# A list scheduler orders all steps of an attention-and-two-MLP kernel; weight splitting and three remainders change engines

## The chip, the cores and the metric

The kernel runs on one core of a Trainium2 chip. The core has engines that each work through an instruction queue of their own, in order: TensorE (PE in the rows; its weight loads are PEld), VectorE (DVE), ScalarE (ACT), GpSimd (POOL) and SyncE (SP, which here only issues DMAs). Semaphores tie the queues together. The metric is the device time of one execution in microseconds (us). The profile gives one execution in detail; its span runs from the first to the last instruction.

## The reference, cut to what matters

```python
# q (1, 12288, 128), kv (1, 384, 32, 128), w_sr (128, 128)
kv_pool = kv.reshape(B, H // r, r, W // r, r, C).mean(axis=(2, 4))      # r = 4
k = v = kv_pool.reshape(B, -1, C) @ w_sr                                 # 768 rows of 128
s = (1.0 / np.sqrt(C)) * (q @ k.transpose(0, 2, 1)); s = s - s.max(-1, keepdims=True)
a = np.exp(s); a /= a.sum(-1, keepdims=True) + 1e-09
x = (a @ v).astype(np.float32).reshape(12288, 128)
h = x @ w_in;  g = np.where(h > 0, h, np.exp(np.minimum(h, 0)) - 1);  x = g @ w_out    # layer 1
h = x @ w_in2; g = np.maximum(0.01 * h, h);                           out = g @ w_out2  # layer 2
```

Both hidden widths are 2048. The weights of the layers are 64-bit floats in the inputs; the kernel reads them as pairs of 32-bit words.

## The kernel before

**Precision.** Every matmul is done three times: each operand is split into a head (a rounded `fp32r` copy) and a tail (the rest), and `mm3` (lines 78 to 81) adds head*head, head*tail and tail*head in PSUM. So each tensor that goes into a matmul has a head (`qh`, `eh`, `xh`, `gh`, `wh`) and a tail (`ql`, `el`, `xl`, `gl`, `wl`), and each tail is a subtraction on VectorE or GpSimd.

**Tiling.** The 12288 rows of q are 24 chunks of 512 columns. For a chunk, four tiles of 128 rows go through `scores` (six matmuls of 384 columns into one PSUM place), the maximum on VectorE, `expo` on ScalarE, `norm` on GpSimd, a write to a DRAM scratch and a read back (`d<-e`, `x<-d`), `turn` (a transpose in blocks on VectorE), and `split_e` (head on ScalarE, tail `el` on GpSimd). Then `values` runs 18 matmuls of 512 columns, and `split_x` makes the chunk's input of layer 1.

A chunk's layer is 8 units of 256 hidden columns. A unit is `up` (six matmuls into a PSUM place of two banks), the activation, `tail`, and `down` (six matmuls that add into the chunk's output bank `py`). In layer 1 the activation is two passes on ScalarE (`r`), then `elu` on VectorE (`g`), which frees the PSUM place, then a head `gh` on GpSimd; in layer 2 it is two passes on ScalarE (`gh` and `g`). `tail` is a subtraction on VectorE in both. There are 384 units. Three PSUM places (`bank2`, one pool of three) serve scores, values and ups in turn; `gl` has three buffers.

**Weights.** 32 blocks of 256 columns are turned from double words into heads and tails by ten steps: a clamp on GpSimd, five bit operations on VectorE, two copies on ScalarE, three products and sums on GpSimd (`split_w`, lines 185 to 232).

**Order.** A tick is one unit. At each tick the loop at the end emits, in a fixed order, `up(n)`, `elu(n-1)`, tails, a share of the weights' steps (all spread over the first `WT = 40` ticks), what the tables `side` and `prod` hold for that tick, the activation, and the `down` of an earlier unit (`LAG`). Units of the two layers alternate from `D2 = 13` units on. Each engine's queue is the order in which this loop emits. Loads go through SP's queue.

## Time and profile before

| what | value |
|---|---|
| median of 3 runs | 1629.83 us (1627.02 to 1638.85) |
| the profiled execution | 1628.08 us, span 1626.3 us |
| TensorE (PE) busy | 1385.2 us, 85% of the span |
| VectorE (DVE) busy | 1200.6 us, 74% |
| ScalarE (ACT) busy | 981.9 us, 60% |
| GpSimd (POOL) busy | 657.1 us, 40% |
| granted TensorE clock, mean | 0.946 |

The first row is the time to be compared, the second the execution from which all rows come; 1.8 us of it lie outside the span. A busy share is a mean over a start that is filled with weight splitting and a long regular stretch, so the stages are to be read apart. A matmul's busy time overlaps the next one's, so the pace of matmuls is read from their starts.

### The profile page before, as it was taken

What the parts mean: (1) busy time and instruction counts of PE and PEld (TensorE: products, weight loads), DVE (VectorE), ACT (ScalarE), POOL (GpSimd) and SP (SyncE); (2) the same over time, 40 slices, a digit from 0 to 9 for tenths busy, and PEclk for the clock granted to TensorE, in tenths of its full rate; (3) what the DMA queues carried; (4) which work ended last, traced back from release to release, by engine and by line L of the source; (5) the groups of instructions that cost most, each with busy time, mean ns of one, the idle gap of its engine ahead of it and who ended that gap; (6) DMA issues with size and microseconds to landing.
All of it is one profiled execution on the core that took longest, in us unless ns stands there. A gap on an engine that the chain in (4) does not pass through costs nothing.

```text
span 1626.3 us, 16605 instructions
## 1 busy us (share of the span) xinstructions
PE 1385.2 (85%) x5688; PEld 1092.7 (67%) x5688; DVE 1200.6 (74%) x1255; ACT 981.9 (60%) x1211; POOL 657.1 (40%) x542
## 2 busy tenths in 40 slices
PE   4356677988998998998999899899899899889998
PEld 3235456766776776776777777677677677767786
DVE  7788877767768778777777677777777777677764
ACT  2343455656657567566566566666666666666665
POOL 3676666334334344343343343443343343343210
PEclk9568788999999999999999899999999999999999
DMA  7432221121121221221221112212222222111100
GB/s 228 126 88 73 71 76 59 55 63 56 55 72 46 65 72 46 66 70 47 65 67 51 55 56 66 60 56 65 52 65 65 53 65 65 46 59 56 36 7 13
DMA packets 176035, 103.91 MB, mean 64 GB/s; under 512 B 105168, under 2 KB 158544, under 8 KB 175952
## 3 DMA queue, kind: packets, MB, share of 16 engines
q1 hardware_dynamic: 174752, 102.66, 22.1%
q8 instruction: 46, 0.75, 0.2%
q10 hardware_dynamic: 1200, 0.20, 0.1%
q14 instruction: 37, 0.30, 0.1%
HBM read 58.79 MB, written 44.04 MB: 63 GB/s over the span
## 4 chain that ended last, share of the span: by engine, by line
PE 48%; DVE 25%; issue 8%; ACT 6%; DMA 2%; POOL 1%; DVEq 0%; SPq 0%; POOLq 0%; ACTq 0%
DVE gl L495 10%; PE ps L79 9%; DVE g L485 8%; PE ps L81 8%; PE ps L80 8%; PE py L80 6%; PE py L79 6%; PE ps L417 6%; PE py L81 5%; DVE nm L354 3%; ACT gh L480 2%; ACT g L481 2%; DMA d<-e 1%; DVE e L395 1%; ACT qh L146 1%
## 5 line engine op out<-in xcount | busy, mean ns | idle before, releaser
L495 DVE TENSOR_TENSOR gl<-g,gh 128x1024 fp32r<-128x1024 f32 x384 | 613.9, 1614 | 351.7 <-ACT g L481 180.2
L489 POOL TENSOR_SCALAR gh<-g 128x1024 fp32r<-128x1024 f32 x192 | 244.0, 1271 | 543.1 <-DVE g L485 506.8
L79 PE MATMUL py<-gh,wh_o 128*128 128x512 f32 x768 | 310.6, 404 | 0.0
L80 PE MATMUL py<-gl,wh_o 128*128 128x512 f32 x768 | 309.6, 403 | 0.0
L81 PE MATMUL py<-gh,wl_o 128*128 128x512 f32 x768 | 308.4, 402 | 0.0
L480 ACT ACTIVATE gh<-ps 128x1024 fp32r<-128x1024 f32 x192 | 196.1, 1021 | 145.1 <-PE ps L81 143.1
L404 POOL TENSOR_TENSOR el<-e,eh 128x768 fp32r<-128x768 f32 x96 | 198.9, 2072 | 174.7 <-ACT eh L403 174.7
L485 DVE SCALAR_TENSOR_TENSOR g<-r,ps 128x1024 f32<-128x1024 f32 x192 | 231.8, 1207 | 10.0 <-ACT r L475 10.0
L360 ACT ACTIVATE e<-ps,nm 128x768 f32<-128x768 f32 x96 | 86.3, 899 | 244.5 <-DVE nm L354 237.3
L79 PE MATMUL ps<-xh,wh_i 128*128 128x512 f32 x384 | 165.5, 431 | 70.5 <-DVE g L485 64.5
L474 ACT ACTIVATE r<-ps 128x1024 f32<-128x1024 f32 x192 | 197.2, 1027 | 33.6 <-PE ps L81 33.6
L475 ACT ACTIVATE r<-r 128x1024 f32<-128x1024 f32 x192 | 203.8, 1062 | 6.1
L481 ACT ACTIVATE g<-ps 128x1024 f32<-128x1024 f32 x192 | 195.8, 1020 | 0.0
L79 PE MATMUL ps<-x2h,wh_i 128*128 128x512 f32 x384 | 154.1, 401 | 42.1 <-DVE g L485 42.1
L81 PEld LDWEIGHTS py<-gh,wl_o 128*128 128x128 f32 x768 | 148.7, 194 | 35.9
L79 PEld LDWEIGHTS py<-gh,wh_o 128*128 128x128 f32 x768 | 150.8, 196 | 32.1
L80 PEld LDWEIGHTS py<-gl,wh_o 128*128 128x128 f32 x768 | 149.2, 194 | 31.7
L80 PE MATMUL ps<-xl,wh_i 128*128 128x512 f32 x384 | 158.7, 413 | 1.1 <-DVE xl L426 1.1
L81 PE MATMUL ps<-xh,wl_i 128*128 128x512 f32 x384 | 158.4, 413 | 0.0
L79 PEld LDWEIGHTS ps<-xh,wh_i 128*128 128x128 f32 x384 | 76.3, 199 | 117.0 <-PE ps L81 48.1
L81 PE MATMUL ps<-x2h,wl_i 128*128 128x512 f32 x384 | 153.9, 401 | 0.0
L80 PE MATMUL ps<-x2l,wh_i 128*128 128x512 f32 x384 | 153.0, 398 | 0.0
(69 smaller groups left out, 1749.0 us busy)
## 6 DMA issues: line engine op xcount, KB each, us to landing
d<-e SPq DMA_DIRECT2D x96, 384.0 KB, 2.5
x<-d SPq DMA_DIRECT2D x96, 384.0 KB, 3.0
qn<-in_q_dram SPq DMA_DIRECT2D x96, 64.0 KB, 2.4
kv<-in_kv_dram SPq DMA_DIRECT2D x12, 512.0 KB, 8.4
out_dram<-y SPq DMA_DIRECT2D x94, 64.0 KB, 2.7
ws<-in_moe_w_in_dram SPq DMA_DIRECT2D x16, 256.0 KB, 2.8
ws<-in_moe_w_out_dram SPq DMA_DIRECT2D x16, 256.0 KB, 2.9
out_dram<-y ACTq DMA_DIRECT2D x2, 64.0 KB, 2.5
```

The lines of the kernel that those rows point to most:

```text
L79: nc.tensor.matmul(ps, w_hi, x_hi, start=start, stop=False)
L80: nc.tensor.matmul(ps, w_hi, x_lo, start=False, stop=False)
L81: nc.tensor.matmul(ps, w_lo, x_hi, start=False, stop=stop)
L404: nc.gpsimd.tensor_tensor(out=lo, in0=e, in1=f(hi), op=ALU.subtract)
L417: nc.tensor.matmul(ps, w, x, start=(i == 0), stop=(i == NMM - 1))
L474: nc.scalar.activation(out=r, in_=ps_u[n], func=AF.Relu, scale=-1.0)
L475: nc.scalar.activation(out=r, in_=r, func=AF.Exp, scale=-1.0)
L480: nc.scalar.activation(out=gh_u[n], in_=ps, func=AF.Prelu, alpha=0.01)
L481: nc.scalar.activation(out=g_u[n], in_=ps, func=AF.Prelu, alpha=0.01)
L485: nc.vector.scalar_tensor_tensor(out=g_u[n], in0=r_u.pop(n), scalar=-1.0, in1=ps_u.pop(n), op0=ALU.add, op1=ALU.max)
L489: nc.gpsimd.tensor_scalar(out=gh_u[n], in0=g_u[n], scalar1=1.0, scalar2=0.0, op0=ALU.mult, op1=ALU.add)
L495: nc.vector.tensor_tensor(out=gl_u[n], in0=g_u.pop(n), in1=f(gh_u[n]), op=ALU.subtract)
```

## The change

All work is written down as steps: an engine, an assumed length, the steps that it comes after, buffers that it takes and gives, and a key (roughly the unit at which it is wanted). A loop in the kernel's Python then keeps an assumed clock for each engine, always emits the step that can begin first (the lower key at equal times, no key more than `REACH = 12` beyond the oldest step left), and so fixes each engine's queue. The three PSUM places are pools of one buffer each, and the loop picks the place that its clock says is free first.

With it: of a weight block's steps, the mask and the product that VectorE did before the shift go; a magnitude (`w_abs`) on ScalarE stands ahead of the clamp, which now bounds from both sides, so VectorE has three operations a block where it had five. Four weight buffers are loaded ahead instead of two. `el` and `ql` are subtracted on VectorE instead of GpSimd. For the first two chunks (`NEARLY = 2`) TensorE transposes the tiles into PSUM and there is no trip through DRAM. `LAG` of layer 2 is 4 (was 3), `D2` is 12, `y` has one buffer (was two), `sums` two (was three).

```diff
-LAG = {1: 4, 2: 3}
-WT = 40
+WS = 4
+D2 = 12
+NEARLY = 2
+LAG = {1: 4, 2: 4}
+AHEAD = 28
+WAHEAD = 6
+REACH = 12
...
-        nc.gpsimd.tensor_tensor(out=lo_v, in0=x, in1=f(hi_v), op=ALU.subtract)
+        nc.vector.tensor_tensor(out=lo, in0=qx.pop(c), in1=f(hi), op=ALU.subtract)
...
-        nc.vector.tensor_scalar(
-            out=u(m), in0=u(v), scalar1=0x7FFFFFFF, scalar2=None, op0=ALU.bitwise_and
-        )
-        yield
-        nc.vector.scalar_tensor_tensor(
-            out=v, in0=m, scalar=LEAST, in1=v, op0=ALU.is_ge, op1=ALU.mult
-        )
+            nc.scalar.activation(out=v, in_=f(wst[i][:, :, 1]), func=AF.Abs)
+            nc.gpsimd.tensor_scalar(
+                out=v, in0=v, scalar1=TOP, scalar2=LEAST, op0=ALU.min, op1=ALU.max
+            )
...
+    def turn_early(t, slot):
+        ps = slot.rearrange("p b n -> p (b n)")
+        e = e_t.pop(t)
+        for b in range(NKB):
+            nc.tensor.transpose(ps[:, b * P:(b + 1) * P], e[:, b * P:(b + 1) * P], ident)
+        e_t[t] = ps[:, :NK].rearrange("p (b s i) -> p b i s", s=S, i=G)
...
+    def tail_e(t):
+        hi, lo = place(t)
+        nc.vector.tensor_tensor(out=lo, in0=e_t.pop(t), in1=f(hi), op=ALU.subtract)
-        nc.gpsimd.tensor_tensor(out=lo, in0=e, in1=f(hi), op=ALU.subtract)
...
+            el = step(DVE, 1.3, lambda n=n: elu(n), [xe], n + 1)
+            gh = step(POOL, 1.1, lambda n=n: elu_head(n), [el], n + 1.5)
+            take(el, "g", n, 3)
+            take(gh, "gh", n, 4)
+            give(el, "ps", u0)
+            both = [el, gh]
...
+                se = step(SP, 0.4, lambda t=t: send(t), [no], key + 3)
+                fe = step(SP, 0.4, lambda t=t: fetch(t), [se], key + 4)
+                tu = step(DVE, 1.0, lambda t=t: turn(t), [fe, av_done.get(c - 1)], key + 5.5)
...
+        tl = chain["tail"] = step(DVE, 1.25, lambda n=n: tail(n), [*both, chain["tail"]], n + 2)
+        take(tl, "gl", n, 3)
...
+    LATE = {ACT: 0.2, DVE: 0.1, POOL: 0.15, PE: 0.25, SP: 4.0}
...
+    while left_n:
+        while begun[left[front][1]]:
+            front += 1
+        horizon = left[front][0] + REACH
+        best = None
+        for e in range(5):
+            for key, i in waiting[e]:
+                if key > horizon:
+                    continue
+                t = can_begin(i)
+                if t is None:
+                    continue
+                t = max(t, ready[i], free_at[e])
+                rank = (max(t, free_at[e] + 0.25), key, i)
+                if best is None or rank < best[0]:
+                    best = rank, t, e, i
```

On VectorE, in the regular stretch, a unit's `elu` (it writes `g`) and the subtractions `gl` stood like this before; the numbers are the buffers, so a `g` can be followed to its `gl`:

```order
L485 SCALAR_TENSOR_TENSOR g_4770<-r_4748,ps_4727 128x1024
L495 TENSOR_TENSOR gl_4785<-g_4775,gh_4774 128x1024
L495 TENSOR_TENSOR gl_4787<-g_4770,gh_4772 128x1024
L354 TENSOR_REDUCE nm_4799<-ps_4792 128x1
L485 SCALAR_TENSOR_TENSOR g_4820<-r_4789,ps_4778 128x1024
L395 STREAM_TRANSPOSE e_4824<-x_4746 128x4x6x32
L495 TENSOR_TENSOR gl_4840<-g_4830,gh_4829 128x1024
L495 TENSOR_TENSOR gl_4842<-g_4820,gh_4822 128x1024
```

The same engine and stretch in the changed kernel:

```order
L402 STREAM_TRANSPOSE e_5055<-x_4865 128x4x6x32
L475 SCALAR_TENSOR_TENSOR g_5066<-r_5041,ps_5032 128x1024
L422 TENSOR_TENSOR el_4846<-e_5055,eh_4845 128x6x128
L402 STREAM_TRANSPOSE e_5086<-x_4999 128x4x6x32
L362 TENSOR_SCALAR ss_5061<-ss_5061 128x1
L363 RECIPROCAL rs_5097<-ss_5061 128x1
L495 TENSOR_TENSOR gl_5102<-g_5066,gh_5072 128x1024
L515 TENSOR_TENSOR x2l_5092<-py_4655,x2h_5091 128x512
L422 TENSOR_TENSOR el_4846<-e_5086,eh_4845 128x6x128
L495 TENSOR_TENSOR gl_5131<-g_5084,gh_5074 128x1024
L475 SCALAR_TENSOR_TENSOR g_5141<-r_5108,ps_5077 128x1024
L347 TENSOR_REDUCE nm_5151<-ps_5117 128x1
```

The subtraction `el` has come into VectorE's queue, and the distance from a `g` to its own `gl` is no longer fixed. Over the whole program the two rows straight behind an `elu` are both `gl` in 67 of 192 places before and in 31 now.

On GpSimd, in the first part of the program (weights of layer 1 and the attention of the first chunks), a stretch read like this before:

```order
L404 TENSOR_TENSOR el<-e,eh 128x6x128
L180 TENSOR_SCALAR v<-ws 128x256
L404 TENSOR_TENSOR el<-e,eh 128x6x128
L227 TENSOR_TENSOR v<-v,m 128x256
L228 TENSOR_TENSOR a<-a,wh_o_1_71 128x256
L229 TENSOR_TENSOR wl_o_1_72<-a,v 128x256
L180 TENSOR_SCALAR v<-ws 128x256
L404 TENSOR_TENSOR el<-e,eh 128x6x128
```

And now, with the same kind of work:

```order
L197 TENSOR_SCALAR v<-v 128x256
L373 TENSOR_SCALAR x<-e,rs 128x768
L197 TENSOR_SCALAR v<-v 128x256
L231 TENSOR_TENSOR v<-v,m 128x256
L373 TENSOR_SCALAR x<-e,rs 128x768
L235 TENSOR_TENSOR a<-a,wh_i_1_63 128x256
L239 TENSOR_TENSOR wl_i_1_64<-a,v 128x256
```

`el` is gone from the queue, and the steps of two blocks stand interleaved. Up to the last weight's tail GpSimd's queue held 128 weight steps, 20 `gh`, 15 `norm`, 14 `el` and 5 `ql` before; now it holds 128 weight steps, 19 `gh` and 16 `norm`. VectorE's queue up to the same block held 160 weight steps before and holds 96 now, with 24 `gl`, 19 `elu`, 17 maxima, 15 `el`, 7 `turn`.

On TensorE, at the end of the first chunk's attention, the order now is:

```order
L88 MATMUL ps_509<-kt_lo_96,qh_420 128x384
L89 MATMUL ps_509<-kt_hi_95,ql_421 128x384
L433 MATMUL ps_530<-eh_438,v_hi_93 128x512 x6
L433 MATMUL ps_530<-eh_438,v_lo_94 128x512 x3
L413 MATMUL ps_551<-ident_60,x_542 128x128 x6
L433 MATMUL ps_530<-eh_438,v_lo_94 128x512 x3
L433 MATMUL ps_530<-el_439,v_hi_93 128x512 x6
```

The six `ident` matmuls are one tile's transposes (48 in all, for eight tiles); between the two halves of `values` before there were scores, and no transposes at all.

## Rows read from the trace of the kernel before

**Rows 1.** Stretches (length, busy and count of each engine, granted clock, DMA).
```profile
0.00:274.50 274.50, 159.26 (x549) 123.73 (x550) 219.65 (x320) 114.78 (x197) 172.11 (x189) 0.78 0.34 104
274.50:1626.30 1351.80, 1225.93 (x5141) 968.93 (x5139) 980.94 (x936) 867.15 (x1015) 485.01 (x354) 0.98 0.20 56
400.00:1400.00 1000.00, 901.95 (x3774) 712.35 (x3775) 742.08 (x713) 642.93 (x761) 379.60 (x276) 0.98 0.21 60
1500.00:1560.00 60.00, 59.55 (x256) 47.42 (x255) 43.31 (x40) 42.11 (x46) 16.36 (x14) 1.00 0.11 31
```
**Rows 2.** Instruction groups on VectorE, 400 to 1400 us (busy us, mean ns, idle before).
```profile
L495 DVE TENSOR_TENSOR gl<-g,gh 128x1024 fp32r<-128x1024 f32 x259 | 431.0, 1678 | 247.5 <-PE py L80 128.4 <-ACT g L481 116.3 <-PE py L81 1.9
L485 DVE SCALAR_TENSOR_TENSOR g<-r,ps 128x1024 f32<-128x1024 f32 x130 | 156.8, 1206 | 0.0
L395 DVE STREAM_TRANSPOSE e<-x 128x768 f32<-128x768 f32 x65 | 63.2, 972 | 8.1 <-DMA x<-d 8.1
L354 DVE TENSOR_REDUCE nm<-ps 128x1 f32<-128x768 f32 x65 | 61.8, 951 | 0.0
```
**Rows 3.** Waits, 400 to 1400 us (who for whom, total, times, longest).
```profile
DVE gl L495 <- PE py L80: 128.4, 66, 4.3
DVE gl L495 <- ACT g L481: 116.3, 91, 3.3
PE ps L79 <- DVE g L485: 98.4, 94, 3.8
```
**Rows 4.** Timeline of TensorE without a gap: first and last of twelve matmuls.
```profile
704.72 0.40 PE L79 MATMUL py<-gh,wh_o 128*128 128x512 f32 x1
...
707.28 0.39 PE L81 MATMUL py<-gh,wl_o 128*128 128x512 f32 x1
```
**Rows 5.** Timeline of GpSimd and VectorE, 703 to 713 us (start, length).
```profile
703.28 1.06 POOL L489 TENSOR_SCALAR gh<-g 128x1024 fp32r<-128x1024 f32 x1 [4.87 <-DVE g L485]
...
707.11 4.02 DVE L495 TENSOR_TENSOR gl<-g,gh 128x1024 fp32r<-128x1024 f32 x2 [2.53 <-ACT g L481]
707.88 2.16 POOL L404 TENSOR_TENSOR el<-e,eh 128x768 fp32r<-128x768 f32 x1 [1.28 <-ACT eh L403]
...
712.43 1.22 DVE L495 TENSOR_TENSOR gl<-g,gh 128x1024 fp32r<-128x1024 f32 x1
712.69 1.87 POOL L489 TENSOR_SCALAR gh<-g 128x1024 fp32r<-128x1024 f32 x1 [0.23 <-DVE g L485]
```
**Rows 6.** Timeline of the start: first weight block, first `values`.
```profile
27.09 0.28 DVE L197 TENSOR_SCALAR m<-v 128x256 uint32<-128x256 uint32 x1
27.41 0.42 DVE L201 SCALAR_TENSOR_TENSOR v<-m,v 128x256 f32<-128x256 f32 x1
30.05 0.72 POOL L227 TENSOR_TENSOR v<-v,m 128x256 f32<-128x256 f32 x1 [6.01 <-DVE m L197]
72.18 1.65 PE L417 MATMUL ps<-eh,v_hi 128*128 128x512 f32 x3 [21.88 <-ACT eh L403]
```
**Rows 7.** Instruction groups of the whole run: weights, `norm`, small matmuls.
```profile
L180 POOL TENSOR_SCALAR v<-ws 128x256 f32<-128x256 f32 x32 | 15.9, 499 | 12.7 <-DMA ws<-in_moe_w_in_dram 5.7 <-DMA ws<-in_moe_w_out_dram 4.9
L227 POOL TENSOR_TENSOR v<-v,m 128x256 f32<-128x256 f32 x32 | 25.8, 806 | 7.5 <-DVE m L197 6.0 <-ACT v L216 1.5
L373 POOL TENSOR_SCALAR e<-e,rs 128x768 f32<-128x768 f32 x96 | 89.9, 937 | 133.9 <-issue 92.8 <-DVE rs L371 37.0 <-ACT r L475 3.6
L212 DVE SCALAR_TENSOR_TENSOR a<-v,a 128x256 uint32<-128x256 uint32 x32 | 25.7, 803 | 0.7
L207 DVE TENSOR_SCALAR a<-v 128x256 uint32<-128x256 uint32 x32 | 21.3, 664 | 0.7
L298 PE MATMUL ps<-pool_m,s 128*128 128x128 f32 x48 | 10.6, 361 | 11.9 <-DVE s L292 11.7
```
**Rows 8.** The exchange through DRAM: DMA issues (count, KB each, median us to landing).
```profile
d<-e SPq DMA_DIRECT2D x96, 384.0 KB, 2.5
x<-d SPq DMA_DIRECT2D x96, 384.0 KB, 3.0
```

More of the change, by code (lines that the diff above doesn't have):

```diff
@@ L232, in split_w @@
-        return rest
-    def split_all():
-        done = None
-        clamp(0)
-        for i in range(len(wjobs)):
-            done = yield from split_w(i, done)
-            yield
-        done()
-    wsteps = split_all()
-    nw = 5 * len(wjobs) + 1
-    wdone = [0]
-    def weights(n, part):
-        due = min(nw, -(-nw * (2 * n + part) // (2 * WT)))
-        while wdone[0] < due:
-            next(wsteps, None)
-            wdone[0] += 1
-    with tc.tile_pool(name="kvp", bufs=1) as kvp, tc.tile_pool(name="sums", bufs=3) as sum_p:
+        return w_abs, w_bound, w_shift, w_sign, w_power, w_low, w_head, w_b, w_rest, w_tail
@@ L255, in pooled_attention_elu_leaky_kernel @@
+    with tc.tile_pool(name="kvp", bufs=1) as kvp, tc.tile_pool(name="sums", bufs=2) as sum_p:
         wsr = kvp.tile([P, C], F32, name="wsr")
@@ L587, in pooled_attention_elu_leaky_kernel, with step, take, give @@
-    assert not later and not side and not prod
+    steps = []
+    takes, gives = {}, {}
+    def step(engine, length, do, after, key):
+        steps.append((engine, length, do, [a for a in after if a is not None], key))
+        return len(steps) - 1
+    def take(i, pool, n, bufs, put=None):
+        takes.setdefault(i, []).append((pool, n, bufs, put))
+    def give(i, pool, n):
+        gives.setdefault(i, []).append((pool, n))
+    PE, DVE, ACT, POOL, SP = range(5)
+    where = {}
+    firsts = {}
@@ new lines, in pooled_attention_elu_leaky_kernel @@
+    LATE = {ACT: 0.2, DVE: 0.1, POOL: 0.15, PE: 0.25, SP: 4.0}
+    count = len(steps)
+    needs = [len(s[3]) for s in steps]
+    feeds = [[] for _ in steps]
+    for i, s in enumerate(steps):
+        for a in s[3]:
+            feeds[a].append(i)
+    ready = [0.0] * count
+    waiting = [[] for _ in range(5)]
+    for i in range(count):
+        if not needs[i]:
+            waiting[steps[i][0]].append((steps[i][4], i))
+    left = sorted((s[4], i) for i, s in enumerate(steps))
+    front = 0
@@ new lines, in pooled_attention_elu_leaky_kernel, with can_begin @@
+    begun = [False] * count
+    free_at = [0.0] * 5
+    order = {}
+    free_from = {}
+    PLACES = 3
+    places = [0.0] * PLACES
+    place_of = {}
+    order["ws"] = list(range(WS))
+    order["e"] = [("q", 0)]
+    free_from["e", ("q", 0)] = 0.0
+    order["qn"] = [0, 1]
+    free_from["qn", 0] = 0.0
+    def can_begin(i):
+        t = 0.0
+        for pool, n, bufs, put in takes.get(i, ()):
+            if pool == "ps":
+                open_ = [x for x in places if x is not None]
+                if not open_:
+                    return None
+                t = max(t, min(open_))
+            else:
+                owners = order.setdefault(pool, [])
+                if len(owners) >= bufs:
+                    x = free_from.get((pool, owners[-bufs]))
+                    if x is None:
+                        return None
+                    t = max(t, x)
+        return t
@@ new lines, in pooled_attention_elu_leaky_kernel @@
+    left_n = count
+    while left_n:
[14 more added lines that the diff above has]
+                    best = rank, t, e, i
+        assert best, "no step can begin"
+        _, t, e, i = best
+        engine, length, do, _, key = steps[i]
+        waiting[e].remove((key, i))
+        begun[i] = True
+        left_n -= 1
+        for pool, n, bufs, put in takes.get(i, ()):
+            if pool == "ps":
+                p = min((x, k) for k, x in enumerate(places) if x is not None)[1]
+                places[p] = None
+                place_of[i] = p
+                put(ps_p[p].tile([P, 2, CH], F32, tag="s", name="ps"))
+            else:
+                order[pool].append(n)
+        do()
+        end = t + length
+        free_at[e] = end
+        seen = end + LATE[e]
+        for pool, n in gives.get(i, ()):
+            if pool == "ps":
+                places[place_of[n]] = seen
+            else:
+                free_from[pool, n] = seen
+        for k in feeds[i]:
+            needs[k] -= 1
+            same = steps[k][0] == e and e != SP
+            ready[k] = max(ready[k], end if same else seen)
+            if not needs[k]:
+                waiting[steps[k][0]].append((steps[k][4], k))
```

504 lines of the change are left out of this document (287 added, 217 removed).

## The prediction

> **What bounds the kernel now.** First the stretches [rows 1]. The run falls into two. Up to 274.5 us, about where the last weight block is finished, TensorE gets through 549 matmuls with busy time 159 us. In the other 1351.8 us it gets through 5141. In the middle of that long part it is the busiest engine, with 902 us in 1000 against VectorE's 742. That share flatters it, because busy times of neighbouring matmuls overlap. Its pace comes from starts without a gap: eleven matmuls of 512 columns in 707.28 - 704.72 = 2.56 us, 0.2327 us each [rows 4]; for 384 columns I take three quarters, 0.1745 us (an estimate by columns). A chunk has 192 matmuls of its 16 units, 18 of `values` and 24 narrow ones of `scores`: 210 x 0.2327 + 24 x 0.1745 = 53.1 us if TensorE never stops. From 400 to 1400 us there are 259 `gl`, 16 a chunk, so 16.2 chunks, 61.7 us each [rows 1, 2]. TensorE runs at 86% of its pace, and 8.6 us a chunk are stalls.
>
> Then who makes it stop. TensorE waits 98.4 us for VectorE's `g`, whose end frees a PSUM place; VectorE waits 128.4 us for TensorE, whose `down` frees a `gl` buffer, and 116.3 us for layer 2's `g` from ScalarE [rows 3]. So the two busiest engines stop each other in turn, though VectorE has work for only 742 of 1000 us: the order of the queues costs the time, not the amount of work. One piece of work does cost: two `gl` take 4.02 us together while GpSimd's `el` runs from 707.88 to 710.04 us, where one alone takes 1.22 us. A `gl` that starts while `el` is on ends about 1.1 us after it. The reverse shows too: `gh` takes 1.06 us alone and 1.87 us when a `gl` began 0.26 us before it [rows 5]. Over the 259 `gl` the mean is 1.678 us, 0.46 above the lone one [rows 2].
>
> **The start.** Both kernels must get 32 weight blocks done and the first chunks through. I measure it to the last weight's tail, and count each queue up to there. VectorE first. Three weight operations cost 0.28 + 0.42 + 0.28 = 0.98 us a block with GpSimd quiet [rows 6], 0.664 + 0.803 + 0.664 = 2.13 us at the run's means [rows 7]: 31 to 68 us. The 24 `gl` at 1.22 to 1.678 us are 29 to 40 us. The 19 `elu` at 1.206 are 23 us, the 17 maxima at 0.951 are 16 us [rows 2]. No row has `el` on VectorE. Its nearest is `gl`, the same subtraction with 1024 columns, so 0.92 to 1.26 us by columns (a gain is excluded, it is new work there): 14 to 19 us for 15. Seven `turn` at 0.97 are 7 us. The short ones and the pieces of 512 columns are some 14 us, an estimate by columns from `gl`. Sum: 134 to 187 us, from 27.1 us on. The two operations that leave VectorE were worth 32 x (0.664 + 0.803) = 47 us at the same means. GpSimd: 32 x (0.499 + 3 x 0.806) = 93 us, 19 `gh` at 1.06 to 1.87 us are 20 to 36 us, 16 `norm` at 0.937 are 15 us, so 128 to 144 us from about 30 us [rows 5 to 7]. VectorE is the longer of the two. Before, VectorE was busy 219.65 of the 274.5 us, 80%, because the ticks doled the weight steps out evenly while the engines waited for each other. With steps taken as they become ready I take 90% busy, between that 80% and full, and the middle of the sum, 160 us: 27 + 160/0.9 = **205 us**. With the low sum it is 175, with the high one 235.
>
> The rest of the start hides. The magnitudes on ScalarE are 32 passes of 256 columns: at GpSimd's 0.72 us for that shape 23 us, and ScalarE was busy for 115 of 274.5 us. If it were the late one, each block would be later by that pass. The 48 transposes cost TensorE between 0.06 us each (a quarter of 0.2327) and 0.361 us [rows 7], 3 to 17 us, while it idles for over 100 us there. They take away four to eight trips through DRAM; the first `values` waited 21.88 us for `eh` at 72.18 us [rows 6]. I count no extra gain, since the weights set the end of the start. Two more weight loads stand ahead of the second chunk's q in SP's queue; q is wanted after the first chunk's scores, so this is nothing, or 2 or 3 us if these loads are slow. One `y` buffer is asked for once a chunk, every 50 us or more; two `sums` buffers feed VectorE while it waits for kv loads: nothing.
>
> A rule of the Trainium skill speaks to this start (SBUF — State Buffer, "Who interferes with whom"): a VectorE operation with two SBUF inputs and a GpSimd operation that reads SBUF exclude each other for the whole of the instruction that came first. The pair at 707 us agrees. By it all such work of both engines would stand in one line: GpSimd's 117 us at the lone prices and VectorE's 70 us make 187 us, the start would end at 27 + 187 = 214 us, and the total would be 9 us longer. No later term uses this.
>
> **The long part.** At the same point of the weights the changed order has done a little less on TensorE: with 20 units of layer 1 and 7 of layer 2 begun, some 5170 matmuls are left (4695 wide, 474 narrow), 1092.5 + 82.7 = 1175 us of pace, or 22.15 chunks; before it was 1168 us in 1351.8.
>
> VectorE's load per chunk is now 8 x 1.206 + 16 x 1.22 + 4 x 0.951 + 4 x 0.972 + 4 x 0.92 (`el`) + about 4 for the small ones = 45 us, if nothing collides. `el` was on GpSimd and held up a `gl` by about 1.66 us (2.88 of the 4.02 against 1.22); now it adds 0.92 us and holds up nobody on TensorE's path by itself. What is left on GpSimd and collides is 8 `gh` and 4 `norm` a chunk. Each can hold VectorE up by its own length at most, 8 x 1.06 + 4 x 0.937 = 12 us, or by nothing when VectorE happens to read PSUM or to transpose. I take half, 6 us: 51 us, under the 53.1 us of TensorE. So TensorE should become the bound, with VectorE close behind. Of the waits, `gl` for layer 2's `g` should go, because a `gl` is placed when its input is due, and so should the stops for PSUM places, because ups and downs alternate. What is late next is VectorE after a collision: I let half of the 6 us reach TensorE, **56.1 us a chunk** (95% of pace; the row for 1500 to 1560 us shows TensorE busy 59.55 of 60 where VectorE has 43 [rows 1], so such a pace exists). 22.15 x 56.1 = 1243 us. `LAG` 4 in layer 2 holds `gh` and `gl` a tick longer; its cover is that VectorE's `gl` comes early, and without it VectorE stops for `gl` as it does now.
>
> Sum: 205 + 1243 + 1.8 outside the span = **1450 us**, 178 less than the profiled execution's 1628.08: 69.5 from the start, 109 from the long part. The median of before is 1.75 us above that execution, far less than the uncertainty, so 1450 stands for the median too.
>
> **Rivals.** (1) The collisions become the bound. Nearly every `gh` meets a `gl` or `el`, VectorE needs 45 + 12 = 57 us and the pace is some 58 us: 205 + 22.15 x 58 + 2 = 1492. For it: two `gl` or an `el` and a `gl` follow straight behind many `elu`, and the mean `gl` was 0.46 us too long. Against: after many `elu` the next one is a maximum or a transpose. [...] (2) The start does not get shorter, since the interlock of weight steps on three engines paces it, not the ticks: 274.5 + 1243 + 2 = 1519. Against: both queues hold far less work than 247 us. (3) The pace stays: `gl` buffers tie VectorE to `down` as now, 61.7 us a chunk, 205 + 1367 + 2 = 1574. Against: the `el` block is gone in any case. (4) Better than I say: collisions mostly miss and the start takes 180 us, at 54 us a chunk: 180 + 1196 + 2 = 1378. (5) Slower than before: the exchange through DRAM. SP's queue is in order; a `fetch` waits there for its `send` to land, and `turn` on VectorE waits for the `fetch` with every `elu` behind it. If each of the 88 tiles left held VectorE and through it TensorE up by w, the time is 1450 + 88 w: slower by over 1% from w = 2.2 us, and 1714 at w = 3. Against it: the trip is 2.5 + 3.0 us and two issues [rows 8], the plan allows 8.8 us for it, and VectorE waited only 8.1 us for 65 of them [rows 2]. That the change does nothing is excluded: the queues show the steps moved.
>
> **How the numbers follow.** Forecast (1400 to 1475 or so) 58%, rival 1 14%, rival 2 8%, rival 3 6%, rival 4 10%, rival 5 4%. The range 1385 to 1535 takes in the forecast, rivals 1 and 2 and the starts of 175 to 235 us; it leaves out most of rival 4 and rivals 3 and 5, about two in ten. Within 1% of 1630 us, which is about what a measurement of this kernel can tell from no change, lies almost nothing: 2%. Faster by more 95%, slower by more 3%.
>
> **What would show it.** In the changed profile: the last weight's tail on GpSimd near 205 us; between 400 and 1400 us 285 `gl` instead of 259; a mean `gl` near 1.35 us; VectorE waiting for ScalarE's and TensorE's `gl` inputs less than half as long; TensorE waiting for `g` under 50 us. It is wrong if `gl` keeps its 1.68 us (rival 1), if weights end after 250 us (rival 2), or if `turn` waits for `x<-d` for over 100 us (rival 5).

## The result and the profile after

The changed kernel takes **1386.61 us** (median of four runs, 1382.48 to 1387.5) against 1628.42 us before: a ratio of 0.8501, interval 0.8458 to 0.8544. The forecast of 1450 us had the sign, the bound and the length of the start right and was 63 us too high, and the time lies at the low edge of its range. The profiled execution took 1382.48 us, its span 1380.7 us.

First the stretches of the changed kernel, in the columns of [rows 1] (length, busy time and count of TensorE, weight loads, VectorE, ScalarE and GpSimd, granted clock, DMA):

```profile
27.10:207.10 180.00, 136.54 (x530) 104.79 (x530) 154.57 (x232) 121.77 (x215) 145.54 (x164) 0.87 0.28 81
207.10:1380.70 1173.60, 1167.93 (x5144) 963.50 (x5142) 948.79 (x1035) 874.86 (x1014) 320.48 (x253) 1.00 0.24 64
300.00:1300.00 1000.00, 1000.00 (x4410) 825.99 (x4409) 825.86 (x910) 753.46 (x880) 284.27 (x224) 1.00 0.25 67
```

207.1 us is the end of the last weight block's tail, a row of GpSimd's timeline:

```profile
205.48 1.62 POOL L239 TENSOR_TENSOR wl_o<-a,v 128x256 fp32r<-128x256 f32 x1
```

So the start fell from 274.5 to 207.1 us, by 67.4 us, and the rest from 1351.8 to 1173.6 us, by 178.2 us. Together this is 245.6 us, the whole difference of the two profiled executions. From 300 to 1300 us TensorE is busy in all of 1000.00 us; before it was 902 [rows 1].

A part of the difference is TensorE's clock, which the prediction did not count. Over the long part before, the granted clock was 0.98 on average [rows 1]: it was 0.50 (1.2 GHz) in short stretches, about 55 us in all, and 1.00 (2.4 GHz) in the rest. One of them in the kernel before (first TensorE's timeline, then the stretch), behind a wait of TensorE for `g`:

```profile
897.55 0.66 PE L79 MATMUL ps<-kt_hi,qh 128*128 128x384 f32 x1 [3.54 <-DVE g L485]
...
900.03 0.63 PE L80 MATMUL py<-gl,wh_o 128*128 128x512 f32 x1
900.46 0.63 PE L81 MATMUL py<-gh,wl_o 128*128 128x512 f32 x1
...
896.20:902.80 6.60, 5.25 (x14) 4.62 (x15) 3.09 (x4) 2.33 (x3) 2.77 (x2) 0.50 0.38 119
```

Wide matmuls start 0.43 us apart there instead of 0.2327 [rows 4]. So some 25 us of the 178 are matmuls at the lower clock (an estimate: 55 x (1 - 0.2327 / 0.43)). In the changed kernel's long part the clock is 1.00. In the start it was 0.78 on average before, and is 0.87 now in the 180 us shown.

Next the instruction groups from 300 to 1300 us, VectorE's and then GpSimd's (busy us, mean ns, idle time before and who ended it), against [rows 2]:

```profile
L495 DVE TENSOR_TENSOR gl<-g,gh 128x1024 fp32r<-128x1024 f32 x304 | 372.3, 1255 | 61.8 <-POOL gh L481 58.1
L475 DVE SCALAR_TENSOR_TENSOR g<-r,ps 128x1024 f32<-128x1024 f32 x152 | 184.4, 1213 | 67.3 <-ACT r L471 67.1
L422 DVE TENSOR_TENSOR el<-e,eh 128x768 fp32r<-128x768 f32 x74 | 83.8, 1132 | 6.7 <-ACT eh L418 6.7
...
L481 POOL TENSOR_SCALAR gh<-g 128x1024 fp32r<-128x1024 f32 x152 | 171.3, 1127 | 566.7 <-DVE g L475 501.3 <-PE ps L89 60.6 <-PE py L88 4.8
L373 POOL TENSOR_SCALAR e<-e,rs 128x768 f32<-128x768 f32 x72 | 113.0, 1569 | 148.1 <-DVE rs L363 76.1 <-ACT x2h L511 35.4 <-ACT r L468 35.3
```

304 `gl` are 19 chunks, 52.6 us each, which is what the expectations below use. By matmuls, 234 a chunk, 4410 are 18.85 chunks and 53.06 us each; the stretch holds the scores of one chunk less than its units, so this is the better pace. `gl` no longer waits for TensorE or for ScalarE's `g`; what ended nearly all of its 61.8 us of idle time is GpSimd's `gh`. It is hardly held up while it runs, either: its mean is 1.255 us where it was 1.678. Last the waits from 400 to 1300 us (total, times, longest), where [rows 3] had TensorE waiting 98.4 us for VectorE's `g`. In the answer for the changed kernel no wait of TensorE's matmuls is left to list:

```profile
POOL gh L481 <- DVE g L475: 451.4, 122, 8.7
ACT r L468 <- PE ps L89: 110.9, 103, 2.2
...
DVE g L475 <- ACT r L471: 60.8, 69, 2.5
...
DVE gl L495 <- POOL gh L481: 52.3, 61, 1.3
```

The other engines wait mostly for TensorE or for what follows from it, and the page's chain of work says the same, with 86% of the span on it where TensorE had 48% before:

```profile
PE 86%; DVE 5%; POOL 4%; issue 2%; ACT 1%; DMA 1%; SPq 0%; DVEq 0%; POOLq 0%; ACTq 0%
```

### The profile page after: what moved, and what is told of

The parts are those of the page before. It is cut to its first block, busy times and chain, and to the rows that moved or that the text cites. A ratio compares the mean times of both kernels' runs of the same rounds, so it can differ in the third digit from the quotient of the medians.

```text
span 1380.7 us, 16414 instructions
## 1 busy us (share of the span) xinstructions
PE 1318.0 (95%) x5736; PEld 1080.2 (78%) x5736; DVE 1120.0 (81%) x1303; ACT 1001.6 (73%) x1243; POOL 466.7 (34%) x422
## 4 chain that ended last, share of the span: by engine, by line
PE 86%; DVE 5%; POOL 4%; issue 2%; ACT 1%; DMA 1%; SPq 0%; DVEq 0%; POOLq 0%; ACTq 0%
PE ps L88 14%; PE ps L87 14%; PE ps L89 14%; PE py L88 12%; PE py L89 12%; PE py L87 12%; PE ps L433 6%; POOL a L235 1%; DVE a L210 1%; POOL v L231 1%; DMA kv<-in_kv_dram 1%; DVE gl L495 1%; POOL wl_i L239 0%; POOL v L197 0%; DVE a L203 0%
## 5 line engine op out<-in xcount | busy, mean ns | idle before, releaser
L495 DVE TENSOR_TENSOR gl<-g,gh 128x1024 fp32r<-128x1024 f32 x384 | 475.2, 1265 | 97.1 <-POOL gh L481 77.5
L481 POOL TENSOR_SCALAR gh<-g 128x1024 fp32r<-128x1024 f32 x192 | 216.9, 1130 | 654.1 <-DVE g L475 580.7
L87 PE MATMUL py<-gh,wh_o 128*128 128x512 f32 x768 | 305.0, 397 | 5.0 <-POOL gh L481 2.9
L475 DVE SCALAR_TENSOR_TENSOR g<-r,ps 128x1024 f32<-128x1024 f32 x192 | 232.7, 1213 | 76.3 <-ACT r L471 76.1
L373 POOL TENSOR_SCALAR e<-e,rs 128x768 f32<-128x768 f32 x88 | 134.1, 1524 | 162.8 <-DVE rs L363 83.6
L88 PEld LDWEIGHTS py<-gl,wh_o 128*128 128x128 f32 x768 | 145.6, 190 | 47.3 <-DVE gl L495 17.6
L87 PEld LDWEIGHTS py<-gh,wh_o 128*128 128x128 f32 x768 | 145.5, 189 | 36.6 <-POOL gh L481 4.1
L87 PE MATMUL ps<-xh,wh_i 128*128 128x512 f32 x384 | 155.4, 405 | 7.7 <-DVE g L475 3.8
L88 PE MATMUL ps<-xl,wh_i 128*128 128x512 f32 x384 | 154.5, 402 | 0.0
L89 PE MATMUL ps<-xh,wl_i 128*128 128x512 f32 x384 | 154.3, 402 | 0.0
L422 DVE TENSOR_TENSOR el<-e,eh 128x768 fp32r<-128x768 f32 x88 | 101.1, 1150 | 8.3 <-ACT eh L418 8.3
```

The lines of the kernel that those rows point to most:

```text
L87: nc.tensor.matmul(ps, w_hi, x_hi, start=start, stop=False)
L88: nc.tensor.matmul(ps, w_hi, x_lo, start=False, stop=False)
L89: nc.tensor.matmul(ps, w_lo, x_hi, start=False, stop=stop)
L373: nc.gpsimd.tensor_scalar(out=x, in0=e, scalar1=rs_t.pop(t), scalar2=1.0, op0=ALU.mult, op1=ALU.mult)
L422: nc.vector.tensor_tensor(out=lo, in0=e_t.pop(t), in1=f(hi), op=ALU.subtract)
L475: nc.vector.scalar_tensor_tensor(out=g_u[n], in0=r_u.pop(n), scalar=-1.0, in1=ps_u.pop(n), op0=ALU.add, op1=ALU.max)
```

## The experiments

Seventeen kernels ran. Ratios are to the kernel before on the same chip, with their 95% intervals, and the medians of before in these batches were 1628.87 to 1632.4 us, so a few us between kernels of different batches are not told apart. Each kernel has one trace. In the short diffs a line without a sign is context, `...` marks a cut, and calls are joined to one line.

### Where the long part's stalls came from

**e8.** The kernel before, with one condition changed: layer 2's `gl` is placed one tick later in VectorE's queue.

```diff
-        if is_unit(n - 1, 2):
-            tail(n - 1)
-        if is_unit(n - 2, 1):
+        if n - 2 in units:
             tail(n - 2)
```

> The kernel before with layer 2's gl taken one tick later (two ticks behind its up, as in layer 1), so that VectorE no longer stands in front of ScalarE's g, for which it waited 116 us in 1000. If that in-line wait is what delays elu and so the PSUM places: 1520 to 1580 us. If it only becomes a wait for a gl buffer or gh: 1600 to 1640 us.

Measured: 1480.74 us, 0.9077 [0.905, 0.9104], 40 us below the range expected. Its stretches:

```profile
274.50:1479.20 1204.70, 1175.57 (x5136) 955.51 (x5136) 831.28 (x936) 867.54 (x1014) 574.40 (x353) 1.00 0.22 63
400.00:1400.00 1000.00, 978.84 (x4284) 796.09 (x4282) 699.87 (x798) 727.25 (x857) 498.85 (x307) 1.00 0.24 66
```

And VectorE's `gl`, GpSimd's `gh` and `el` in its instruction groups from 300 to 1300 us, then `gh` and `el` of the kernel before in the same window:

```profile
L495 DVE TENSOR_TENSOR gl<-g,gh 128x1024 fp32r<-128x1024 f32 x293 | 355.6, 1214 | 59.0 <-POOL gh L489 57.9
L489 POOL TENSOR_SCALAR gh<-g 128x1024 fp32r<-128x1024 f32 x146 | 272.9, 1869 | 349.5 <-DVE g L485 349.5
L404 POOL TENSOR_TENSOR el<-e,eh 128x768 fp32r<-128x768 f32 x74 | 139.2, 1881 | 123.9 <-ACT eh L403 95.0 <-DVE gl L495 27.2 <-DVE ss L370 1.7
...
L489 POOL TENSOR_SCALAR gh<-g 128x1024 fp32r<-128x1024 f32 x129 | 161.9, 1255 | 382.4 <-DVE g L485 379.1 <-PE ps L81 3.3
L404 POOL TENSOR_TENSOR el<-e,eh 128x768 fp32r<-128x768 f32 x65 | 137.9, 2121 | 129.5 <-ACT eh L403 129.5
```

The part behind 274.5 us takes 1204.7 us instead of 1351.8: moving this one place in the queue is worth 147 us, against 178 for the whole change. (The gains of e8, e7 and e2 in the old order overlap and cannot be added.) VectorE had stood in line for a `g` that ScalarE was still writing, with ready work behind it. All that the prediction found wrong with `gl` goes with it: the wait for ScalarE's `g`, the wait for `down`, and the block by GpSimd's `el`. `el` still runs on GpSimd here, but `gl` no longer meets it: its mean is 1.214 us. What loses now is GpSimd's `gh`, with 1.869 us where it took 1.255.

**e2.** The kernel before, with `el` and `ql` on VectorE, in the old order.

```diff
-        nc.gpsimd.tensor_tensor(out=lo_v, in0=x, in1=f(hi_v), op=ALU.subtract)
+        nc.vector.tensor_tensor(out=lo_v, in0=x, in1=f(hi_v), op=ALU.subtract)
...
-        nc.gpsimd.tensor_tensor(out=lo, in0=e, in1=f(hi), op=ALU.subtract)
+        nc.vector.tensor_tensor(out=lo, in0=e, in1=f(hi), op=ALU.subtract)
```

> The kernel before, in its ticks, with el and ql on VectorE and nothing else changed. Theory A: the queues still stop each other, and at most the 1.66 us per el comes back, 4 a chunk against 0.92 us of new work, so 0 to 4 us of 61.7 us a chunk: 1540 to 1630 us. Rival B: the pace falls to about 53 us a chunk, 1410 to 1450 us.

Measured: 1584.94 us, 0.9713 [0.9677, 0.9749]. The mean `gl` falls to 1.236 us, but the idle time ahead of it stays what it was:

```profile
L495 DVE TENSOR_TENSOR gl<-g,gh 128x1024 fp32r<-128x1024 f32 x268 | 327.5, 1236 | 250.5 <-ACT g L481 130.7 <-PE py L80 114.5 <-PE py L81 4.9
```

So taking `el` and `ql` off GpSimd was worth 1632.09 - 1584.94 = 47 us in the old order, and the one place of e8 three times that.

**e7.** The kernel before with a fourth `gl` buffer.

```diff
-    gl_p = pool("gl", 3)
+    gl_p = pool("gl", 4)
```

> The kernel before with a fourth gl buffer and nothing else. VectorE waited 128 us in 1000 for a gl buffer. If that wait is one link of a ring that holds TensorE up: the pace falls from 61.7 to 58 us a chunk or less, 1550 us or less. If the wait only moves to the next link (layer 2's g from ScalarE, the PSUM places): 1600 to 1630 us.

Measured: 1555.42 us, 0.9538 [0.9506, 0.9569], between the expectations. The wait for `down` is gone, the one for ScalarE's `g` is not; a fourth buffer treats one symptom:

```profile
L495 DVE TENSOR_TENSOR gl<-g,gh 128x1024 fp32r<-128x1024 f32 x274 | 459.6, 1708 | 166.9 <-ACT g L481 134.6 <-POOL gh L489 32.3
```

**e5.** The changed kernel with the old `LAG` of layer 2, so that TensorE's queue has two downs and then two ups, as before, instead of an up and a down in turn.

```diff
-LAG = {1: 4, 2: 4}
+LAG = {1: 4, 2: 3}
```

> The changed kernel with the lag of layer 2's down at 3 again. TensorE's queue then has two downs and two ups in a row, as in the kernel before, and the scheduler still places all else. If the alternation of down and up is what keeps PSUM places and gl buffers free in time: the pace rises to 55 us a chunk or more, 1430 us or more. If it is the placing of VectorE's and ScalarE's work: 1380 to 1400 us.

Measured: 1387.56 us, 0.8509 [0.848, 0.8538], the time of the changed kernel. The stops for PSUM places did not come back: from 300 to 1300 us TensorE is busy for 993.49 us and waits for `e` for 6.1 us and for `g` for 2.2. That ups and downs alternate is therefore not why they went. It may still be worth something: this kernel has the shorter of the two matmul steps described below throughout, the changed kernel mostly the longer one, and against e14, which has the shorter one too, it is 16 us slower.

**e6.** The changed kernel, in which the scheduler takes 0.85 us for every step of VectorE, ScalarE and GpSimd.

```diff
+        length = length if engine in (PE, SP) else 0.85
```

> The changed kernel, but the scheduler is told 0.85 us for every step of VectorE, ScalarE and GpSimd, whatever it is. If the keys and the lists of needs make the order: 1385 to 1410 us. If the lengths that the scheduler assumes must be close to the measured ones: over 1430 us.

Measured: 1417.91 us, 0.8694 [0.8669, 0.8719], between the expectations. From 300 to 1300 us TensorE is busy for 979.22 us instead of 1000, 295 `gl` are done, and `gl` waits 110.7 us for `gh`. Assumed lengths near the measured ones are worth 31 us in time (46 against e14, which has the same matmul step, see below). Without them the change still gives 1631.48 - 1417.91 = 214 us.

### What collisions cost

**e1.** The changed kernel with `el` (from the third chunk on) and `ql` back on GpSimd.

```diff
+        (nc.vector if t // NJ < NEARLY else nc.gpsimd).tensor_tensor(
...
+            te = step(*((DVE, 1.0) if early else (POOL, 1.9)), lambda t=t: tail_e(t), [he], key + 6.5)
...
+            q_ready[c + 1] = step(POOL, 1.25, lambda c=c: tail_q(c + 1), [hq], end + 1.4)
```

> The changed kernel with el and ql subtracted on GpSimd again from the third chunk on (the list scheduler is told 1.9 and 1.25 us for them). Theory A (the order of the queues took the stalls away, and GpSimd and VectorE have room to spare): VectorE loses 4 x 1.13 us of el a chunk and gets back up to 4 x 1.66 us of blocked gl, so the pace stays within 1.5 us of 52.6 us a chunk and the time is 1390 to 1425 us. Rival B (el's block of VectorE set the pace): most of the old pace of 61.7 us returns, 1500 to 1590 us.

Measured: 1392.88 us, 0.8533 [0.8513, 0.8554], 6 us above the changed kernel and in theory A's range:

```profile
300.00:1300.00 1000.00, 988.08 (x4377) 812.66 (x4376) 784.93 (x814) 745.95 (x875) 424.77 (x315) 1.00 0.25 67
L497 DVE TENSOR_TENSOR gl<-g,gh 128x1024 fp32r<-128x1024 f32 x301 | 424.4, 1440 | 145.0 <-POOL gh L483 134.2 <-PE py L88 10.8
...
L422 POOL TENSOR_TENSOR el<-e,eh 128x768 fp32r<-128x768 f32 x74 | 161.4, 2182 | 129.1 <-ACT eh L418 129.1
```

The collisions are back (`gl` 0.185 us longer, `el` 2.182 us), and TensorE stops for 12 of 1000 us. The 6 us understate that: e1 has the shorter matmul step throughout and the changed kernel mostly the longer one (below). Against e14, which has the shorter one too, e1 is 21 us slower, 1 us a chunk.

**e4.** The changed kernel, with `gl` of every second unit of layer 1 done twice: 4 x 1.22 = 4.9 us more work for VectorE a chunk.

```diff
...
+        if units[n][0] == 1 and units[n][2] % 2 == 0:
+            nc.vector.tensor_tensor(out=gl_u[n], in0=g_u[n], in1=f(gh_u[n]), op=ALU.subtract)
```

> The changed kernel with the subtraction gl of every second layer-1 unit done twice (the same result again), not told to the scheduler: 4 x 1.22 = 4.9 us more of VectorE a chunk. If VectorE's lateness is hidden as long as it has room (43.5 us of work in 52.6): 1383 to 1400 us. If half of what VectorE loses reaches TensorE, as the prediction had it: 22 x 2.4 us more, about 1440 us.

Measured: 1422.31 us, 0.8712 [0.8692, 0.8733], between the expectations. Its stretch, and the one long wait of TensorE's matmuls in it:

```profile
300.00:1300.00 1000.00, 976.77 (x4306) 799.72 (x4306) 904.12 (x974) 735.87 (x866) 267.45 (x222) 1.00 0.25 68
...
PE py L87 <- DVE x2l L520: 21.2, 19, 1.6
```

With 4306 matmuls, 18.40 chunks, VectorE has 904.12 / 18.40 = 49.1 us of work a chunk, and a chunk takes 54.3 us, 1.3 more than in the changed kernel. But e4 too has the shorter matmul step throughout (below). So has e14, and its stretch, shown there, gives 52.5 us a chunk without the added matmuls. At the same step, then, about 1.9 of the 4.9 us come through, most of it in one wait a chunk, for layer 2's `x2l` from VectorE.

### The start

**e9.** The first two chunks go through DRAM as before.

```diff
-NEARLY = 2
+NEARLY = 0
```

> The changed kernel with all chunks sent through DRAM (NEARLY = 0), no transposes on TensorE. If the weights alone set the end of the start, as the prediction had it: 1383 to 1395 us. If the first chunk's attention is part of it (the first values waited until 72 us in the kernel before): 10 to 30 us more, 1396 to 1420 us.

Measured: 1389.99 us, 0.8521 [0.8487, 0.8554]. The last weight tail begins at 215.40 us instead of 205.48, so the transposes bring the end of the weights forward by 10 us, though the prediction gave them nothing. In the time it is 3 us, which is not clear of the spread between batches; in this trace the longer matmul step ends at 1213 us, which gives some of it back.

**e12.** The five VectorE operations a weight block, and no magnitude on ScalarE.

```diff
-            nc.scalar.activation(out=v, in_=f(wst[i][:, :, 1]), func=AF.Abs)
+            nc.gpsimd.tensor_scalar(
+                out=v, in0=f(wst[i][:, :, 1]), scalar1=TOP, scalar2=-TOP, op0=ALU.min, op1=ALU.max
+            )
...
+            nc.vector.tensor_scalar(
+                out=u(m), in0=u(v), scalar1=0x7FFFFFFF, scalar2=None, op0=ALU.bitwise_and
+            )
...
+            nc.vector.scalar_tensor_tensor(
+                out=v, in0=m, scalar=LEAST, in1=v, op0=ALU.is_ge, op1=ALU.mult
+            )
```

> The changed kernel with the old weight steps: five operations on VectorE, clamp straight from the loaded words, no magnitude on ScalarE. The two operations were priced at 47 us of VectorE at the means of the run before. If VectorE is the long queue of the start as the prediction had it: 20 to 50 us more, 1407 to 1437 us. If GpSimd's queue sets it: 1384 to 1396 us.

Measured: 1405.39 us, 0.8612 [0.8582, 0.8641], 19 us above the changed kernel, just below the 1407 to 1437 us expected if VectorE is the long queue and well above the range for GpSimd. All of it is lost ahead of 250 us, by when 682 matmuls are done instead of 784; from 300 to 1300 us both kernels do 4410. The two operations take VectorE 32 x (0.444 + 0.685) = 36 us in this run, and the weights end at 229.4 us instead of 207.1.

**e3.** The scheduler with the old placement of `el` and `ql` and the old weight steps (the edits of e1 and e12 together).

> The list scheduler with the old placement: el and ql on GpSimd from the third chunk on, the weights' five operations on VectorE and no magnitude on ScalarE; only the early transposes stay. Theory A: a pace of 53 to 55 us a chunk and a start that is longer by the 47 us of VectorE's weight operations at most, 1400 to 1480 us, so the order alone is worth over 150 of the 242 us. Rival B: 1520 us or more.

Measured: 1416.86 us, 0.8679 [0.8659, 0.8699]. The order (with the early transposes) gives 1632.09 - 1416.86 = 215 us of the 242 or so, within theory A. It leaves 30 us, or 45 against e14, which has e3's matmul step (below); e1 and e12 together make 25 us, or 40 with e1 set against e14. The weights end at 235.3 us here, so 39 of the start's 67 us come with the order, the transposes and the buffers. The change also has three sets of weight working buffers instead of two, which no run tests by itself.

### What sets the pace when TensorE never waits

**e10, e11.** The changed kernel with two other values of `D2`, by how many units layer 2 runs behind layer 1.

```diff
-D2 = 12
+D2 = 15
...
-D2 = 12
+D2 = 10
```

> The changed kernel with layer 2 beginning 15 units after layer 1 instead of 12, so that layer 2's weights are wanted later and TensorE has three more units without them. If the start is bound by the weights' work: 1372 to 1384 us. If it is bound by all of VectorE's and GpSimd's work whatever the order: 1384 to 1392 us.

> The same knob the other way, layer 2 begins 10 units after layer 1. Weights bind: 1388 to 1400 us. All of the work binds: 1382 to 1390 us.

Measured: 1399.26 us, 0.8569 [0.8542, 0.8597], and 1375.62 us, 0.843 [0.8405, 0.8455]. Both theories had the direction wrong. D2 = 15 stops TensorE briefly (busy 987.87 of 1000 us, 4359 matmuls instead of 4410). But D2 = 10 is 11 us faster although TensorE is busy for only 996.00 us of that stretch, so a longer or shorter wait can't explain it. The timeline of TensorE in the changed kernel does (start, length); first and last of 29 wide matmuls, the seam, first and last of 18:

```profile
509.40 0.39 PE L87 MATMUL py<-gh,wh_o 128*128 128x512 f32 x1
...
515.82 0.39 PE L88 MATMUL py<-gl,wh_o 128*128 128x512 f32 x1
516.05 0.42 PE L89 MATMUL py<-gh,wl_o 128*128 128x512 f32 x1
516.30 0.40 PE L87 MATMUL ps<-xh,wh_i 128*128 128x512 f32 x1
...
520.27 0.39 PE L89 MATMUL ps<-x2h,wl_i 128*128 128x512 f32 x1
```

Up to 515.82 us a step is 6.42 / 28 = 0.2293 us; from 516.30 us on it is 3.97 / 17 = 0.2335 us (0.2333 as a mean over 20 us), and so it stays up to the end. TensorE waits in neither part, and the granted clock is 1.00 in both, by the stretches of this kernel on either side:

```profile
300.00:515.00 215.00, 215.00 (x964) 178.99 (x963) 182.04 (x202) 164.22 (x193) 62.25 (x49) 1.00 0.27 73
517.00:900.00 383.00, 383.00 (x1686) 316.13 (x1685) 319.21 (x356) 287.16 (x338) 112.41 (x88) 1.00 0.26 70
```

Of matmuls of all widths these are 4.48 and 4.40 a microsecond. The long step costs 1.8%, 16 us over these 864 us. With D2 = 10 it begins near 530 us and is over at 624 us, behind a stop of TensorE for layer 2's tail:

```profile
623.91 0.34 PE L89 MATMUL ps<-kt_hi,ql 128*128 128x384 f32 x1
624.42 0.47 PE L87 MATMUL py<-gh,wh_o 128*128 128x512 f32 x1 [0.18 <-DVE x2l L515]
```

Of the other kernels in the scheduler's order, those whose TensorE stops now and then (e1, e3, e4, e5, e6) have the short step in all stretches of 50 or 60 us from 300 us on, a mean of 0.2288 to 0.2294 us between starts, and D2 = 15 nearly throughout; e9 and e12 stop almost nowhere and have the long one from about 526 and 486 us, e9 until 1213 us. So a kernel of the first group, set against the changed kernel, looks up to 16 us better than its stops alone would make it. The kernels in the old order (before, e2, e7, e8) have 0.232 to 0.233 us in all four stretches looked at.

**e13.** The changed kernel with a matmul of 128 columns behind layer 2's tail of three chunks.

```diff
...
+        if c in (9, 14, 19):
+            nc.tensor.matmul(py[:, :P], wblk("i2", 0)[0], lo[:, :P], start=True, stop=True)
```

> The changed kernel, with one added matmul of 128 columns behind layer 2's x tail of chunks 9, 14 and 19: it reads that tail, so TensorE must wait there for ScalarE's head and VectorE's tail, an estimated 1 to 3 us each time (0.7 us for the tail, about as much for the head, and the queues). Its result goes into a PSUM place that is not read any more. Theory (a stop brings the short step back): the step between wide matmuls is 0.2333 us before a stop and 0.229 us behind it, as seen at 624 us with D2 = 10. The changed kernel spends some 864 us in the long step, 1.8% or 16 us too long; with most of that back and 3 to 9 us paid for the stops, 1376 to 1384 us. Rival (the step changes for another reason, and D2 acts through the order): the step stays at 0.2333 us behind the stops, and the time is 1387 plus 3 to 9, so 1390 to 1396 us.

Measured: 1380.03 us, 0.8462 [0.8433, 0.849]. The tails were done in time, so the three hardly stopped TensorE (0.1 us of idle time in all). In the trace the long step comes at 673 us; the second added matmul, at 878.46 us, leaves it; behind the third it is gone:

```profile
1143.58 0.40 PE L88 MATMUL ps<-x2l,wh_i 128*128 128x512 f32 x1
1143.81 0.40 PE L89 MATMUL ps<-x2h,wl_i 128*128 128x512 f32 x1
1144.04 0.40 PE L87 MATMUL ps<-x2h,wh_i 128*128 128x512 f32 x1
1144.28 0.40 PE L88 MATMUL ps<-x2l,wh_i 128*128 128x512 f32 x1
1144.51 0.39 PE L89 MATMUL ps<-x2h,wl_i 128*128 128x512 f32 x1
1144.85 0.33 PE L518 MATMUL py<-x2l,wh_i 128*128 128x128 f32 x1
```

From 1160 us to the end, all stretches of 20 us have a mean of 0.2288 to 0.2292 us. The time is the one that the theory expected, but its mechanism is too narrow: a disturbance can bring the short step back without being a real stop, and not each one does.

**e14.** The same narrow matmul, without anything to wait for, ahead of layer 1's first `down` in each of the 24 chunks; the next matmul starts its PSUM place anew.

```diff
+            if m == 1:
+                nc.tensor.matmul(yps[m, c][:, :P], wblk("o1", 0)[0], gh_u[n][:, 0, :P], start=True, stop=True)
```

> The changed kernel, with one added matmul of 128 columns ahead of the first down matmul of layer 1 in each chunk (24 in all); its operands are there already, so TensorE does not wait for it, and the next matmul starts its PSUM place anew. Theory (only a stop brings the short step back): the step goes to 0.2333 us near 517 us as before and stays, and the time is 1386.6 plus 24 x 0.06 to 0.23, so 1388 to 1392 us. Rival (any break in the regular row of shapes brings it back): the step is 0.229 us nearly throughout and the time is 1371 to 1378 us.

Measured: **1371.65 us**, 0.8403 [0.8374, 0.8432], the fastest of all. The theory that only a stop helps falls; the rival was right. The step is 0.2289 to 0.2295 us in every stretch of 20 us, and TensorE does 70 matmuls more in the same 1000 us, 19 of them the added ones, so the others make 4461 / 234 = 19.06 chunks of 52.5 us:

```profile
300.00:1300.00 1000.00, 1000.00 (x4480) 833.63 (x4479) 833.03 (x917) 761.93 (x889) 287.50 (x227) 1.00 0.24 67
```

**e15, e16, e17.** Two more values of `D2` in the changed kernel, and a third in e14's kernel.

```diff
-D2 = 12
+D2 = 11
...
-D2 = 12
+D2 = 8
...
-D2 = 12
+D2 = 10
```

> The changed kernel with D2 = 11. Theory (D2 acts through the step): the time follows the microseconds spent in the long step, at 1.8% of them, from about 1371 us with none; if TensorE never stops, as with 12, it is 1383 to 1388 us, and if layer 2's x tail stops it for a moment every other chunk, as with 10, 1373 to 1379 us; trace and time go together. Rival (D2 acts through the order and the end of the run, 5.5 us for each unit between 10 and 12): 1381 us whatever the step does.

> The changed kernel with D2 = 8, so that layer 2 of a chunk follows right behind its layer 1. Theory (D2 acts through the step): the short step stays, since TensorE now stops for layer 2's x tail once a chunk, but each of these stops costs: the head and the tail are some 1.5 us and the two units of cover are gone, so 0.5 to 3 us in each of 22 chunks and 1375 + 11 to 66 = 1386 to 1441 us. Rival (5.5 us for each unit, through a shorter end of the run): 1364 us.

> The changed kernel with D2 = 10 and with the added matmul of 128 columns of e14 in each chunk. Theory (between 10 and 12, D2 acts only through the step between wide matmuls): the step is 0.229 us throughout, as with D2 = 12 and this matmul, so the time is that kernel's 1371.65 us, plus the moments in which layer 2's x tail stops TensorE every other chunk with D2 = 10 (11 of 0.1 to 0.5 us): 1371 to 1377 us. Rival (D2 acts through the order and the end of the run as well, 5.5 us a unit): 11 us below 1371.65, so 1359 to 1363 us.

Measured: 1373.47 us, 0.8418 [0.8389, 0.8446]; 1401.11 us, 0.8588 [0.856, 0.8617]; and 1378.62 us, 0.8461 [0.8428, 0.8493]. D2 = 11 has the long step in parts of 680 to 980 us only and lies where the share says, not at the rival's 1381. D2 = 8 keeps TensorE busy for 981.04 of 1000 us only, with 16.2 us of waits for `x2l`, as expected; but its step does not stay short, as the theory had it: it is 0.2333 us from about 916 to 963, 1078 to 1125, 1175 to 1230 and 1242 to 1280 us, although TensorE stops once a chunk. In e17 the long step comes and goes once in two chunks (0.2333 us from 430 to 460 us, from 535 to 565 and so on, a quarter of the time in all), and TensorE waits 4.2 us for `x2l`; the time missed the theory's 1371 to 1377 by 1.6 us and the rival's 1359 to 1363 by far. That D2 acts through the end of the run at 5.5 us a unit is out; that this matmul, or a stop, always keeps the short step is out too.

## Why the prediction was right or wrong

**What bounds it, and what the order does: right.** TensorE became the bound, its waits for `g` went from 98.4 us to none, and `gl`'s waits for ScalarE's `g` and for `down` went altogether. Of the reason given, that each queue stops the other, e8 shows the root: layer 2's `gl` standing in VectorE's queue ahead of its input. The other half of the reason, that ups and downs alternate, is not needed for it (e5). Not all of the 8.6 us a chunk that it called stalls were stalls: about 1.1 us (25 us over 22 chunks, an estimate) were matmuls at the lower clock, which went with the stops.

**The start, 205 us: 207.1 measured, in part by luck.** VectorE's work was put at 160 us and 90% busy; the trace has 154.57 in the 180 us behind 27.1, 86%. That VectorE's work matters there is shown by e12. But two sizes inside were off. The two weight operations that left VectorE were worth 19 us (e12), not 47: they take 36 us in that run, less than at the run's means of [rows 7], and not all of it reaches the end. And the transposes, put at "no extra gain", bring the end of the weights forward by 10 us (e9). The 160 us are the middle of a sum from 134 to 187, and the 90% was a choice; that both came out near is not shown to be more than chance.

**The long part, 1243 us: wrong by 69 us, and this is the term that failed.** "I take half, 6 us", and "I let half of the 6 us reach TensorE", made 56.1 us a chunk. Measured over the long part it is 1173.6 us for 5144 matmuls, by the prediction's count of 5170 for 22.15 chunks 22.04 chunks, so 53.25 us. That is 22.04 x 2.85 = 63 us of the 69; the other 6 are the 26 matmuls fewer. The timeline in [rows 5] shows both directions, a `gl` held up by `el` and a `gh` held up by a `gl`, and the term put all collisions on VectorE. In the new order GpSimd loses. VectorE pays 16 x (1.255 - 1.22) + 4 x (1.132 - 0.92) = 1.4 us a chunk, GpSimd's `norm` 4 x (1.569 - 0.937) = 2.5 us and `gh` 8 x (1.127 - 1.06) = 0.5 us, and GpSimd is busy for 284 of 1000 us, so that its loss does not show on TensorE, which is busy throughout. VectorE's load is 825.86 / 18.85 = 43.8 us a chunk instead of 51. So the step that failed is the size of the collisions, 1.4 us a chunk for the 6 us taken. The other factor, that half of VectorE's loss reaches TensorE, is not what failed: where VectorE really has 49 us of work (e4), about two fifths of what is added do. With 1.4 us in place of 6 the same sum gives 53.8 us a chunk and, over 22.04 chunks, some 1393 us. The better case (rival 4) had the pace almost right with its 54 us, and took the start for shorter than it is. Of the signs named, a mean `gl` near 1.35 us came out at 1.255.

**The pace without stops, 53.1 us: right by chance.** It rested on one step of 0.2327 us [rows 4]. The changed kernel has two, 0.2293 and 0.2335 us, which make 210 x 0.2293 + 24 x 0.172 = 52.3 and 210 x 0.2335 + 24 x 0.175 = 53.2 us (the 384-column steps at three quarters); the traced run is in the long one for 864 us.

**The exchange through DRAM** (rival 5) did not show: VectorE's `turn` waits 0.3 us for `x<-d` in the whole run.

**Open:** what sends TensorE into the long step, and why one narrow matmul ends it and another doesn't. The runs exclude the granted clock (1.00 in both), longer waits (none is listed in either) and the chip (both steps occur in one execution). At the seam the weight load of 516.10 us begins 0.05 us behind the matmul ahead of it and not at once; at 463.81 us the same load is 0.04 us late, and the step does not change. So a late load alone does not explain it. That the long step is 16 us of the changed kernel's time rests on the step's length times its stretches in one trace, and on e14, whose 15 us of gain fit it.

## What to carry to other kernels

In an in-order queue, look first for the instruction that stands there before its input is due: one such place was worth 147 us here, more than any tested change of what work is done where. When two engines exclude each other, work out which of them will be second in the new order, and whether that one has room, before pricing the collision. And once the bounding engine never waits, its time per instruction is the next thing to read, in several stretches of the run, since 2% can sit there where busy time says 100%, and can hide what an experiment costs.
